# Two attention and FFN layers of a decode step: load sizes changed, and the last mean taken through the row sums of w_o

## Chip, core and metric

One core of a Trainium2 chip. The metric is the device time of one execution in microseconds (us). Engines are named as in the profile: PE (TensorE), PEld (its weight loads), DVE (VectorE), ACT (ScalarE), POOL (GpSimd), SP (SyncE, which issues all loads).

## The reference, cut to what matters

```python
def _layernorm(x, axis=-1, eps=1e-5):
    m = jnp.mean(x, axis=axis, keepdims=True); v = jnp.var(x, axis=axis, keepdims=True)
    return (x - m) / jnp.sqrt(v + eps)
def _A_ref(x, k_cache, v_cache, wq, wo):     # B=4, D=512, 32 heads, 8 KV heads, S=8192, Dh=128
    q = (x @ wq) as heads; k, v = each KV head repeated 4 times
    p = softmax(q k^T * Dh**-0.5);  return (p v, heads joined) @ wo
def _B_ref(x, w_gate, w_up, w_down):         # F=1792
    return (silu(x @ w_gate) * (x @ w_up)) @ w_down
x = x + _A_ref(_layernorm(x), ...);  x = x + _B_ref(_layernorm(x), ...)
x = x + _A_ref(_layernorm(x), ...);  x = x + _B_ref(_layernorm(x), ...)
```

Both layers use the same caches and weights. Everything is bf16, one token for each of 4 batches.

## The kernel before, in words

A unit is one KV head of one batch: 2 MB of K and 2 MB of V. There are 32 units a layer. On-chip memory has 8 slots of 2 MB (`kvf`, lines 202 to 203); layer 1 begins with the three units whose K and V are still there from layer 0 (`NRES`), so 122 caches of 2 MB are loaded in all. The list `items` (335 to 346) is the order of all loads, and `pump` (391) issues the next one on SP's queue as soon as its slot is free. Most caches come in one load of 2 MB. Those in `fours` (351) come in quarters of 512 KB: the last unit of each layer and the units 3 to 5 of layer 1's order, K and V both.

For each unit `keys` turns K in eight blocks (`turn`, DVE), makes the scores in eight blocks on PE (`scores`), and queues the softmax steps in the list `line`; `values` makes the products with V and queues what follows in the list `after`. Both lists are worked off between blocks (`advance`, `flush`). The last unit of a layer has V in the roles of weights, in eight blocks (`block_last`, 651): each block of 8 products waits for the piece of V it is in. Ahead of the last but one block the two lists are flushed (657 to 659): the row sums of p (`total`), and the rows of the unit before (`add_rows`, a product on PE and a step `scale_o` on DVE).

At the end of a layer `out_proj` (699) puts x into a PSUM bank by an identity product (`x_ahead`), picks the heads into `o4` and adds the 16 products with w_o. Then `center` (735) reduces the new x over its four column groups on DVE (`vs`), sums over the partitions by a product with ones into the bank `LNB`, and subtracts the mean from x (`xn`). `warm` puts in products whose result nobody reads. `ffn` (816) makes gate and up (4 x 14 products each), the activation, and down.

The FFN weights lie in slots 6 and 7 and a little room behind them. w_down comes in seven blocks of 256 rows (387); a partition gets 2 consecutive rows, so the columns of gate and up are taken in steps of 2 elements (833 and 834). In layer 0, as `ffn` has used a quarter slot's worth of weights, it issues the next quarter of the two K that follow (841 to 843, 884 to 895). In layer 1 the first two units' K slots are handed on by `quarter` (436): after every second score block (564) a quarter of the load that comes next into that slot is issued. For layer 1 the last quarters of w_gate and w_up are kept on chip (`park`, `keep`, `kept_at`) and the first three of w_up stay where they are, so only three quarters of w_gate and w_down are loaded again.

PE's, DVE's and ACT's instructions are recorded in program order and played at the end (`roll`, 898), with the repeating middle of a layer in a hardware loop; each engine runs its own list in order.

Of the kernel before, what the change touches and what calls it, by code (L numbers as in the profile page):

```python
# [146 lines left out]
def bass_interleave_layers__gqa_block_cached__swiglu_ffn__decode_kernel(  # L147
# [45 lines left out]
    with ExitStack() as es:  # L193
# [18 lines left out]
        wd_sb = kvf[:, f1:f1 + FO * D].rearrange("p (f n) -> p f n", f=FO)  # L212
        places = [f"s{s}.{q}" for s in range(NKEEP, NSLOT) for q in range(NB)]
        room = lambda a, b: places[(a - f0) // (TB * Dh):(b - 1 - f0) // (TB * Dh) + 1]
        at_w = {"wg": room(f0, f0 + FR * F), "wg3": room(f2, f2 + F), "wu": room(f3, f3 + F),
                **{("wd", j): room(f1 + 2 * j * D, f1 + (2 * j + 2) * D) + [f"wd{j}"] for j in range(FO // 2)}}
# [13 lines left out]
        rstd = sb("rstd", [P, B], FP32)  # L230
        o4 = sb("o4", [P, REP, B], BF16)
# [31 lines left out]
        def few(ap):  # L263
# [13 lines left out]
        sem_l = [sem(f"sem_l{q}") for q in range(NQ)]  # L277
        sem_h = [[sem(f"sem_h{k}{i}") for i in range(NQ)] for k in range(2)]
        sem_p = [sem(f"sem_p{i}") for i in range(7)]
        sem_x = sem("sem_x")  # L280
        sem_w = {n: [sem(f"sem_{n}{i}") for i in range(c)]
                 for n, c in (("wq", KT), ("wo", 1), ("wg", KT), ("wu", KT), ("wd", FO // 2))}
# [68 lines left out]
        fours = {(L, unit_order[L][-1]) for L in range(2)} | {(1, u) for u in unit_order[1][NRES:2 * NRES]}  # L351
# [19 lines left out]
        def load_weight(name, i=0):  # L371
# [11 lines left out]
            elif name == "wu":  # L383
                for k in range(KT):
                    T.dma("sp", [(wu_sb[k], runs(B_w_up[k * P:(k + 1) * P, :]))], sem_w["wu"][k], writes=[f"wu{k}"])
            else:
                for j in range(FO // 2):
                    T.dma("sp", [(wd_sb[:, 2 * j:2 * j + 2, :].rearrange("p e n -> p (e n)"),
                                  runs(B_w_down[2 * j * P:(2 * j + 2) * P, :]))], sem_w["wd"][j], writes=[f"wd{j}"])

        def pump():
            while issued[0] < len(items):
# [19 lines left out]
                if it in split:  # L412
                    n = NB // NQ
                    for q in range(NQ):
                        part(it, s, q * n, (q + 1) * n, sem_l[q])
                elif (L, u) in fours:
                    part(it, s, 0, NB, sem_s[s])
# [3 lines left out]

        def part(it, s, a, b, sem_):
            kind, L, u = it
            assert (L, u) in fours
            n = NB // NQ
            w, m = n * TB * Dh, S // NQ
            src = (A_k_cache if kind == "K" else A_v_cache)[u % B, u // B, :, :]
            T.dma("sp", [(kv[:, s, q * w:(q + 1) * w], runs(src[q * m:(q + 1) * m, :])) for q in range(a // n, b // n)],
                  sem_, writes=[f"s{s}.{k}" for k in range(a, b)])
# [6 lines left out]
        def quarter(it, i):  # L436
            to = heirs[it]
            if i == 0:
                place(to, slot_of[it])
            n = NB // NQ  # L440
            part(to, slot_of[it], i * n, (i + 1) * n, sem_h[unit_order[1].index(it[2])][i])

        def finished(it):
# [5 lines left out]
            elif it in heirs:  # L449
                quarter(it, NQ - 1)  # L450
# [102 lines left out]
        def keys(L, u):  # L553
            def block(q):
# [9 lines left out]
                if ("K", L, u) in heirs and (q + 1) % (NB // NQ) == 0 and q < NB - 1:  # L564
                    quarter(("K", L, u), q // (NB // NQ))
# [10 lines left out]
            if (L, i) == (1, B - 1):  # L576
                steps = steps[2:]
            ahead = unit_order[1][i + 2] if L == 1 and i in (1, 2) else u
# [8 lines left out]
        def values(L, u):  # L587
# [63 lines left out]
            def block_last(q):  # L651
# [5 lines left out]
                if q == NB - 2:  # L657
                    flush(line)
                    flush(after)
                warm({NB - 4: 3, NB - 2: 2}.get(q, 0), spare)  # L660
# [21 lines left out]
            if all((L, g * B + k) in done for k in range(B)):  # L682
                rest.append([0.5, None, lambda: out_proj(g, u != unit_order[L][-1])])
                if u != unit_order[L][-1]:
                    rest.append([1.3, None, add_to_x])


# [11 lines left out]
        def out_proj(g, more):  # L699
# [18 lines left out]
            for nt in range(KT):  # L718
                for c in range(REP):
# [3 lines left out]
                         stop=(c == REP - 1 if more else nt * REP + c == KT * REP - 1))  # L723

# [10 lines left out]
        def center(n, m, made=None):  # L735
            src, key = (xT[:], "x") if made is None else (bank(made)[:, 0:XB], f"pb{made}")
            T.op("dve", lambda e: e.tensor_reduce(vs[:], src.rearrange("p (k b) -> p b k", b=B), AX.X, ALU.add),
                 reads=[key], writes=["vs"])
# [3 lines left out]
            T.pe(bank(LNB)[:, 0:B], ones, vs[:], start=True, stop=True,  # L742
# [278 lines left out]
```

## Time and profile before

| | us |
|---|---|
| Median of 3 runs (lowest to highest) | 644.43 (643.29 to 644.66) |
| The profiled execution, its own time | 644.37 |
| Its span in the profile | 642.5 |
| PE, PEld, DVE, ACT, POOL busy | 515.2, 334.9, 450.7, 122.0, 19.3 |
| DMA: moved, mean rate over the span | 273.30 MB, 425 GB/s |
| Loads of 2048 KB: count, issue to landing (K, V) | 56 and 56, 28.9 and 32.7 |
| Loads of 512 KB of K and V: count, issue to landing | 20 and 20, 8.4 and 11.6 |
| Loads of w_down, 256 KB: count, issue to landing | 14, 18.3 |

The DMA row of the page gives the busy share of the 16 DMA engines in 40 slices of 16 us each. A timeline line has start, length, engine, line of the code, operation, written tile <- read tile with shapes, count, and in brackets the idle time ahead with what ended it. The helpers at lines 100, 118 and 136 record nearly all PE, DVE/ACT and DMA instructions, so one tells them apart by tiles and not by lines. The trace also has landing records: a load reports from each of the 16 DMA engines, and has landed with the last report.

### The profile page before, as it was taken

To read this page: it belongs to the slowest core of one execution; us is meant where nothing else is said; L and a number is where in the kernel's file an instruction comes from. 1 tells how busy PE (TensorE), PEld (TensorE's weight loads), DVE (VectorE), ACT (ScalarE), POOL (GpSimd) and SP (SyncE) were. 2 spreads that over 40 slices of the span, in tenths; PEclk is the share of its full clock that TensorE was granted. 3 is DMA by queue.
4 is the path that set the end of the run, shared out by engine and by line. 5 is a ranking of instruction groups with operands and counts; after the bars stand their busy time and mean duration, and the time that the engine had idled before them with its cause. 6 is when DMAs were issued, how large, how long until landed. Compare 5 with 4: busy or idle time off the path is not lost.

```text
span 642.5 us, 13067 instructions
## 1 busy us (share of the span) xinstructions
PE 515.2 (80%) x5063; PEld 334.9 (52%) x5086; DVE 450.7 (70%) x1108; ACT 122.0 (19%) x401; POOL 19.3 (3%) x73
## 2 busy tenths in 40 slices
PE   1656797887979878797888889897868968988987
PEld 1424454554646545455556656564545535645655
DVE  2646666867867767768764759987776876758883
ACT  0111211212212212212221422221221221212222
POOL 0000000000000000000000000000000000000000
PEclk9977789978887897979998999998987989769799
DMA  8999999999999999999999999999999999999996
GB/s 351 433 423 428 440 431 428 435 433 435 429 437 430 433 430 437 429 435 430 433 419 420 423 435 429 430 436 428 433 433 439 428 430 433 439 428 433 424 430 287
DMA packets 12695, 273.30 MB, mean 425 GB/s; under 512 B 3032, under 2 KB 3040, under 8 KB 3040
## 3 DMA queue, kind: packets, MB, share of 16 engines
q1 hardware_dynamic: 12672, 272.98, 99.1%
q8 instruction: 16, 0.26, 0.2%
q14 instruction: 7, 0.06, 0.0%
HBM read 272.96 MB, written 0.00 MB: 425 GB/s over the span
## 4 chain that ended last, share of the span: by engine, by line
DMA 71%; PE 15%; DVE 9%; SPq 4%; issue 1%; ACT 0%; POOL 0%; DVEq 0%; POOLq 0%
DMA kvf<-in_A_k_cache_dram 57%; PE ps L100 15%; DMA kvf<-in_A_v_cache_dram 11%; DVE kvf L118 6%; SPq L136 4%; DMA kvf<-in_B_w_down_dram 2%; DVE acc L118 2%; DVE one L118 1%; DVE pT L118 0%; DVE m L118 0%; ACT pb L118 0%; POOL zq L492 0%; DVE oT L118 0%; ACT one L118 0%; SPq L134 0%
## 5 line engine op out<-in xcount | busy, mean ns | idle before, releaser
L118 DVE STREAM_TRANSPOSE kvf<-kvf 128x512 f32<-128x512 f32 x488 | 322.6, 686 | 87.1 <-DMA kvf<-in_A_k_cache_dram 87.1
L100 PE MATMUL ps<-kvf,zq 128*128 128x256 bf16 x2048 | 316.4, 297 | 16.6 <-DVE kvf L118 11.9
L100 PEld LDWEIGHTS ps<-kvf,zq 128*128 128x128 bf16 x2048 | 197.5, 108 | 78.3 <-DVE kvf L118 28.7
L118 ACT ACTIVATE pb<-m 1x128 f32<-1x128 f32 x64 | 19.7, 308 | 434.4 <-DVE m L118 434.1
L100 PE MATMUL ps<-kvf,pT 128*16 128x512 bf16 x992 | 66.6, 390 | 10.5 <-DVE rl L118 7.5
L118 DVE SCALAR_TENSOR_TENSOR acc<-ps,own,acc 128x128 f32<-128x128 f32 x186 | 65.2, 351 | 5.4 <-ACT acc L118 0.6
L100 PE MATMUL ps<-identf,one 128*1 128x128 f32 x64 | 17.6, 275 | 49.0 <-DVE one L118 48.8
L100 PEld LDWEIGHTS ps<-identf,one 128*1 128x1 f32 x64 | 5.1, 80 | 77.3 <-DVE one L118 72.9
L100 PEld LDWEIGHTS ps<-kvf,pT 128*16 128x16 bf16 x992 | 19.4, 89 | 40.0 <-issue 22.3
L118 DVE TENSOR_REDUCE one<-ps 128x1 f32<-128x256 f32 x64 | 26.0, 406 | 18.5 <-PE ps L100 18.3
L118 ACT ACTIVATE pb<-ps,one,rstd 128x256 bf16<-128x256 f32 x64 | 36.0, 563 | 2.1
L100 PEld LDWEIGHTS ps<-head,acc 128*128 128x128 f32 x124 | 21.5, 217 | 28.2 <-DVE acc L118 26.3
L492 POOL TENSOR_TENSOR zq<-scr,quad 128x64 bf16<-128x64 bf16 x62 | 18.1, 292 | 599.6 <-PE ps L100 478.5
L100 PE MATMUL ps<-head,acc 128*128 128x4 f32 x124 | 24.2, 266 | 14.8 <-DVE acc L118 14.7
L118 DVE RECIPROCAL rl<-ps 128x4 f32<-128x4 f32 x64 | 10.4, 163 | 35.4 <-PE ps L100 35.4
L100 PEld LDWEIGHTS ps<-one,pb 1*128 1x128 f32 x128 | 21.3, 207 | 26.3 <-ACT pb L118 22.8
L100 PE MATMUL ps<-one,pb 1*128 1x1 f32 x128 | 26.8, 276 | 9.1 <-ACT pb L118 9.1
L118 DVE STREAM_TRANSPOSE pT<-pb 128x256 bf16<-128x256 bf16 x64 | 26.0, 407 | 4.6 <-ACT pb L118 4.5
L100 PE MATMUL ps<-wq_sb 128*128 128x512 bf16 (+1 forms) x83 | 27.3, 399 | 2.0 <-issue 1.3
L100 PE MATMUL ps<-xn,wq_sb 128*128 128x32 bf16 x284 | 21.1, 181 | 6.6 <-DMA wq_sb<-in_A_wq_dram 6.0
L100 PEld LDWEIGHTS ps<-rsm,one 128*128 128x128 f32 x128 | 22.0, 215 | 4.0 <-ACT rsm L118 2.5
L100 PEld LDWEIGHTS ps<-o,wo_sb 128*128 (+1 forms) x256 | 19.7, 101 | 8.3 <-issue 4.6
(72 smaller groups left out, 254.7 us busy)
## 6 DMA issues: line engine op xcount, KB each, us to landing
kvf<-in_A_k_cache_dram SPq DMA_DIRECT2D x56, 2048.0 KB, 28.9
kvf<-in_A_v_cache_dram SPq DMA_DIRECT2D x56, 2048.0 KB, 32.7
kvf<-in_A_k_cache_dram SPq DMA_DIRECT2D x20, 512.0 KB, 8.4
kvf<-in_A_v_cache_dram SPq DMA_DIRECT2D x20, 512.0 KB, 11.6
wq_sb<-in_A_wq_dram SPq DMA_DIRECT2D x4, 1024.0 KB, 8.2
wo_sb<-in_A_wo_dram SPq DMA_DIRECT2D x8, 512.0 KB, 37.6
kvf<-in_B_w_down_dram SPq DMA_DIRECT2D x14, 256.0 KB, 18.3
kvf<-in_B_w_gate_dram SPq DMA_DIRECT2D x7, 448.0 KB, 17.9
```

Of the source, the lines that this page charges most:

```text
L100: return e.matmul(out, lhsT=lhsT if at is None else lhsT(place(at)), rhs=rhs, **kw)
L118: self.tape[engname].append((repr((name, args, kw)), lambda e, _: getattr(e, name)(*args, **kw), left, sig, None))
L136: ins = e.add_instruction(mybir.InstDMACopy(name=self.nc.get_next_instruction_name(), mode="Copy", queue="qSPDynamicHW", ins=e.lower_ap_dm ...
L492: T.op(eng, lambda e: e.tensor_tensor(dst, q4, m4_, ALU.mult), reads=keys_ + ["quad"], writes=["zq"])
```

## The change

**Loads.** A table `pieces` takes the place of `fours`: units 3 to 5 of layer 1 come in two halves of 1 MB (K and V), the last unit of layer 0 in a half and two quarters, the last of layer 1 in three quarters and two eighths. `quarter` becomes `succeed`, which issues a piece when the score blocks that lay in its room are done; in `ffn`, `give` does it by the weights' room. w_down comes in five blocks (4, 4, 4, 1 and 1 groups of 128 rows) in place of seven; a partition then gets 4 consecutive rows in the first three, and gate and up take their columns in steps of 4 elements there and of 1 in the last two.

**The last mean.** For layer 1 alone. In layer 0's `ffn` ACT sums the rows of w_o that belong to the last KV head (`sum_rows`, 4 instructions), and DVE splits the f32 sums in three bf16 parts (`split_sums`, 7 instructions, in layer 1 at its fifth unit). At the last but one V block `mean_ahead` reduces x as it is before the last projection and multiplies by ones into `LNB`; behind w_o's 16 products `mean_rest` adds 12 products of the parts, each as a column repeated 128 times, with `o4`. `center` then leaves out its reduction and its product with ones, and has one warming product of 256 columns in place of two of 512.

```diff
@@ -210,10 +210,14 @@
...
+        WD = [(0, 4), (4, 8), (8, 12), (12, 13), (13, 14)]
+        assert WD[-1][1] == FO
+        wd_of = lambda fo: next(j for j, (a, b) in enumerate(WD) if a <= fo < b)
         places = [f"s{s}.{q}" for s in range(NKEEP, NSLOT) for q in range(NB)]
...
         at_w = {"wg": room(f0, f0 + FR * F), "wg3": room(f2, f2 + F), "wu": room(f3, f3 + F),
-                **{("wd", j): room(f1 + 2 * j * D, f1 + (2 * j + 2) * D) + [f"wd{j}"] for j in range(FO // 2)}}
+                **{("wd", j): room(f1 + a * D, f1 + b * D) + [f"wd{j}"] for j, (a, b) in enumerate(WD)}}
         wq_sb = sb("wq_sb", [P, KT, HqDh], BF16)
@@ -228,6 +232,9 @@
...
+        ws = sb("ws", [P, 2, REP], FP32)
+        ws3 = sb("ws3", [P, 3, REP], BF16)
         o4 = sb("o4", [P, REP, B], BF16)
@@ -348,7 +355,9 @@
...
         heirs = {("K", 1, unit_order[1][k]): items[ends[0] + 3 + k] for k in range(2)}
-        fours = {(L, unit_order[L][-1]) for L in range(2)} | {(1, u) for u in unit_order[1][NRES:2 * NRES]}
...
+        pieces = {(0, unit_order[0][-1]): (4, 2, 2), (1, unit_order[1][-1]): (2, 2, 2, 1, 1),
+                  **{(1, u): (4, 4) for u in unit_order[1][NRES:2 * NRES]}}
         issued = [0]
@@ -384,9 +393,9 @@
...
             else:
-                for j in range(FO // 2):
-                    T.dma("sp", [(wd_sb[:, 2 * j:2 * j + 2, :].rearrange("p e n -> p (e n)"),
-                                  runs(B_w_down[2 * j * P:(2 * j + 2) * P, :]))], sem_w["wd"][j], writes=[f"wd{j}"])
+                for j, (a, b) in enumerate(WD):
+                    T.dma("sp", [(wd_sb[:, a:b, :].rearrange("p e n -> p (e n)"), runs(B_w_down[a * P:b * P, :]))],
+                          sem_w["wd"][j], writes=[f"wd{j}"])
@@ -410,35 +419,39 @@
...
                 if it in split:
-                    n = NB // NQ
-                    for q in range(NQ):
-                        part(it, s, q * n, (q + 1) * n, sem_l[q])
-                elif (L, u) in fours:
-                    part(it, s, 0, NB, sem_s[s])
+                    for i in range(len(pieces[L, u])):
+                        part(it, s, i, i + 1, sem_l[i])
+                elif (L, u) in pieces:
+                    part(it, s, 0, len(pieces[L, u]), sem_s[s])
                 else:
...
+        def bounds(it, i):
+            n = pieces[it[1:]]
+            return sum(n[:i]), sum(n[:i + 1])
...
             kind, L, u = it
-            assert (L, u) in fours
-            n = NB // NQ
-            w, m = n * TB * Dh, S // NQ
             src = (A_k_cache if kind == "K" else A_v_cache)[u % B, u // B, :, :]
-            T.dma("sp", [(kv[:, s, q * w:(q + 1) * w], runs(src[q * m:(q + 1) * m, :])) for q in range(a // n, b // n)],
-                  sem_, writes=[f"s{s}.{k}" for k in range(a, b)])
+            w, m = TB * Dh, S // NB
+            at = [bounds(it, i) for i in range(a, b)]
+            T.dma("sp", [(kv[:, s, c * w:d * w], runs(src[c * m:d * m, :])) for c, d in at], sem_,
+                  writes=[f"s{s}.{k}" for c, d in at for k in range(c, d)])
...
-        def quarter(it, i):
+        def succeed(it, k):
...
             to = heirs[it]
-            if i == 0:
+            if to not in slot_of:
                 place(to, slot_of[it])
-            n = NB // NQ
-            part(to, slot_of[it], i * n, (i + 1) * n, sem_h[unit_order[1].index(it[2])][i])
+            for i in range(len(pieces[to[1:]])):
+                if bounds(to, i)[1] == k + 1:
+                    part(to, slot_of[it], i, i + 1, sem_h[unit_order[1].index(it[2])][i])
@@ -561,8 +574,8 @@
...
                     deviation(lsc_sb, "lsc")
-                if ("K", L, u) in heirs and (q + 1) % (NB // NQ) == 0 and q < NB - 1:
-                    quarter(("K", L, u), q // (NB // NQ))
+                if ("K", L, u) in heirs and q < NB - 1:
+                    succeed(("K", L, u), q)
                 if q == NB // NQ and L == 1 and first:
@@ -575,6 +588,8 @@
...
                 steps = steps[2:]
+            if (L, i) == (1, B):
+                split_sums()
             ahead = unit_order[1][i + 2] if L == 1 and i in (1, 2) else u
@@ -657,6 +672,8 @@
...
                     flush(after)
+                    if L == 1:
+                        mean_ahead()
                 warm({NB - 4: 3, NB - 2: 2}.get(q, 0), spare)
@@ -680,10 +697,38 @@
...
             if all((L, g * B + k) in done for k in range(B)):
-                rest.append([0.5, None, lambda: out_proj(g, u != unit_order[L][-1])])
+                rest.append([0.5, None, lambda: out_proj(g, u != unit_order[L][-1], L == 1)])
                 if u != unit_order[L][-1]:
...
+        def sum_rows(g):
+            for c in range(REP):
+                T.op("act", lambda e: e.activation(bank(TOT)[:, 0:D], wo_sb[:, g, c, :], ACTF.Copy, accum_out=ws[:, 0, c:c + 1]),
+                     reads=["wo3"], writes=[f"pb{TOT}", "ws"])
...
+        def split_sums():
...
+            left, part_ = ws[:, 0, :], ws[:, 1, :]
+            for k in range(3):
+                T.op("dve", lambda e: e.tensor_copy(ws3[:, k, :], left), reads=["ws"], writes=["ws3"])
+                if k < 2:
+                    T.op("dve", lambda e: e.tensor_copy(part_, ws3[:, k, :]), reads=["ws3"], writes=["wsp"])
+                    T.op("dve", lambda e: e.tensor_tensor(left, left, part_, ALU.subtract), reads=["ws", "wsp"], writes=["ws"])
...
+        def mean_ahead():
...
+            T.op("dve", lambda e: e.tensor_reduce(vs[:], xT[:].rearrange("p (k b) -> p b k", b=B), AX.X, ALU.add),
+                 reads=["x"], writes=["vs"])
+            T.pe(bank(LNB)[:, 0:B], ones, vs[:], start=True, stop=False, reads=["vs", "onesf"], writes=[f"pb{LNB}"])
...
+        def mean_rest():
...
+            for k in range(3):
+                for c in range(REP):
+                    T.pe(bank(LNB)[:, 0:B], ws3[:, k, c:c + 1].to_broadcast([P, P]), o4[:, c, :], start=False,
+                         stop=(k == 2 and c == REP - 1), reads=["ws3", "o4"], writes=[f"pb{LNB}"],
+                         sig=(k == 2 and c == REP - 1))
@@ -721,6 +766,8 @@
...
                          stop=(c == REP - 1 if more else nt * REP + c == KT * REP - 1))
+            if sums and not more:
+                mean_rest()
@@ -732,15 +779,17 @@
...
-        def center(n, m, made=None):
+        def center(n, m, made=None, summed=False):
             src, key = (xT[:], "x") if made is None else (bank(made)[:, 0:XB], f"pb{made}")
-            T.op("dve", lambda e: e.tensor_reduce(vs[:], src.rearrange("p (k b) -> p b k", b=B), AX.X, ALU.add),
-                 reads=[key], writes=["vs"])
+            if not summed:
+                T.op("dve", lambda e: e.tensor_reduce(vs[:], src.rearrange("p (k b) -> p b k", b=B), AX.X, ALU.add),
+                     reads=[key], writes=["vs"])
             if made is not None:
...
             warm(m, SBK[0])
-            T.pe(bank(LNB)[:, 0:B], ones, vs[:], start=True, stop=True,
-                 reads=["vs", "onesf"], writes=[f"pb{LNB}"])
+            if not summed:
+                T.pe(bank(LNB)[:, 0:B], ones, vs[:], start=True, stop=True,
+                     reads=["vs", "onesf"], writes=[f"pb{LNB}"])
             warm(n, SBK[0])
@@ -787,11 +836,11 @@
...
-        def kept_at(name, f=None):
+        def kept_at(name, f=None, n=1):
...
             a = {"wg": 0, "wu": G - 1}[name] * w
-            return a if f is None else wq_sb[:, f // w, a + f % w:a + f % w + 2 * P - 1:2]
+            return a if f is None else wq_sb[:, f // w, a + f % w:a + f % w + n * (P - 1) + 1:n]
@@ -820,8 +869,16 @@
...
             ks = items[ends[0] + 1:ends[0] + 3]
-            n = NB // NQ
-            size = n * TB * Dh
+            rooms = [(k, NKEEP + n, i, n * SL + bounds(k, i)[1] * TB * Dh) for n, k in enumerate(ks)
+                     for i in range(len(pieces[k[1:]]))]
...
+            def give(a, b):
...
+                for n, (k, s, i, end) in enumerate(rooms):
+                    if a < end <= b:
+                        if i == 0:
+                            place(k, s)
+                        part(k, s, i, i + 1, sem_p[n])
             for (w_sb, wname, bk) in ((wg_sb, "wg", gb), (wu_sb, "wu", ub)):
@@ -830,8 +887,9 @@
...
                     for fo in range(FO):
-                        f = fo // 2 * 2 * P + fo % 2
-                        w = kept_at(wname, f) if kt == FR and last else w_sb[kt][:, f:f + 2 * P - 1:2]
+                        a, b = WD[wd_of(fo)]
+                        f, n = a * P + fo - a, b - a
+                        w = kept_at(wname, f, n) if kt == FR and last else w_sb[kt][:, f:f + n * (P - 1) + 1:n]
                         T.pe(out[:, fo, :, :], w, few(xn[:, kt * B:(kt + 1) * B]),
@@ -839,8 +897,7 @@
...
                 if bk == gb and not last:
-                    place(ks[0], NKEEP)
-                    part(ks[0], NKEEP, 0, (f1 - f0) // size * n, sem_p[0])
+                    give(0, f1 - f0)
             T.op("dve", lambda e: e.tensor_tensor(fb(gr), fb(gT), rb, ALU.mult),
@@ -867,7 +924,7 @@
...
                              start=(fo == i == 0), stop=(fo == (BOTH if i == 2 else FO) - 1),
-                             reads=["hT"] + at_w["wd", fo // 2], writes=[f"pb{k}"], sig=(fo == (BOTH if i == 2 else FO) - 1))
+                             reads=["hT"] + at_w["wd", wd_of(fo)], writes=[f"pb{k}"], sig=(fo == (BOTH if i == 2 else FO) - 1))
                     if fo == BOTH - 1:
@@ -875,24 +932,16 @@
...
             park("wg")
+            sum_rows(unit_order[1][-1] // B)
             for fo in range(FO):
...
                          start=False, stop=(fo == FO - 1 and nt == KT - 1),
-                         reads=["hT"] + at_w["wd", fo // 2], writes=[f"pb{OUTB}"], sig=(nt == KT - 1 and fo % 2 == 1))
-                i = (f1 - f0 + (fo + 1) * D) // size
-                if i > (f1 - f0 + fo * D) // size:
...
-                    if i <= NQ:
-                        part(ks[0], NKEEP, (i - 1) * n, i * n, sem_p[i - 2])
-                        if i == NQ:
-                            place(ks[1], NKEEP + 1)
-                    else:
-                        part(ks[1], NKEEP + 1, (i - NQ - 1) * n, (i - NQ) * n, sem_p[i - 2])
-                        if fo == FO - 1:
-                            part(ks[1], NKEEP + 1, (i - NQ) * n, (i - NQ + 1) * n, sem_p[5])
-                            part(ks[1], NKEEP + 1, NB - n, NB, sem_p[6])
+                         reads=["hT"] + at_w["wd", wd_of(fo)], writes=[f"pb{OUTB}"], sig=(nt == KT - 1 and fo % 2 == 1))
+                at = f1 - f0 + fo * D
+                give(at, at + D)
+            give(at + D, 2 * SL)
@@ -979,7 +1028,10 @@
...
             flush(after)
-            center(2, 2, OUTB)
+            if L == 1:
+                center(0, 1, OUTB, True)
+            else:
+                center(2, 2, OUTB)
             rows = ffn(L == 1)
```

## The prediction

> **What bounds the kernel now.** I read the page's slices and DMA queues first, then the windows of 20 us, then the chain of the last 60 us, then the timeline of the last 12. The DMA row and its queue say that the 16 DMA engines are never idle:
>
> ```profile
> DMA  8999999999999999999999999999999999999996
> GB/s 351 433 423 428 440 431 428 435 433 435 429 437 430 433 430 437 429 435 430 433 419 420 423 435 429 430 436 428 433 433 439 428 430 433 439 428 433 424 430 287
> ...
> q1 hardware_dynamic: 12672, 272.98, 99.1%
> q8 instruction: 16, 0.26, 0.2%
> ```
>
> The reader sees 99.1% of the span in packets of one queue, and a dip to 419 to 423 GB/s in slices 21 to 23 (321 to 369 us), the change of layers, where the 512 KB and 256 KB pieces are. So before the last loads only a cheaper stream of transfers can save time: an engine that works there is covered. The chain of the end says where that stops:
>
> ```profile
> 614.42 16.40 DMA kvf<-in_A_v_cache_dram
> 630.82 0.05 issue
> 630.87 2.49 PE ps L100 x55
> 633.36 0.02 issue
> 633.38 0.19 DVE o L118
> 633.57 0.04 issue
> 633.61 0.79 PE ps L100 x17
> 634.40 0.04 issue
> 634.45 0.62 PE ps L100 x3
> 635.07 0.16 issue
> 635.22 5.13 PE ps L100 x141
> ```
>
> From 630.82, when the third quarter of the last V lands, to 642.5 it is TensorE and short VectorE steps, not DMA. The fourth quarter lands at 632.04 by the landing records. The last w_down pair lands at 639.69 and is used at about 640.1, so the weights are not late.
>
> **Own time.** The profiled execution took 644.37 us, of which the span is 642.5; the median shown is 644.43 (643.29 to 644.66), so the two agree. I make the sum against 644.37. About 0.2%, 1.3 us, is what a measurement of this kernel can tell from no change.
>
> **Term 1, the loads.** 191 transfers become 175. Up to the third quarter of the last V there are 15 fewer: 12 in the six units of layer 1 (quarters to halves), 2 in layer 0's last K and V, 2 in layer 0's w_down, and one more in layer 1's last K. What one costs I take from the landing records, by the last engine to report. Whole 2 MB loads land every 4.847 us (418.63 to 602.82 in 38 steps), quarters every 1.227 (351.36 to 368.54 in 14), so 4.908 a unit: three more transfers cost 0.061, 0.020 each. Six units give -0.25, layer 0's last pair -0.04, the last K +0.02. w_down's 256 KB blocks land every 0.627; three of 512 KB at 1.227 and two of 128 KB at 0.327 (half the step from 512 to 256 taken off 0.627, an estimate) make 4.34 in place of 4.39: -0.05. Sum **-0.32**. The other end is the packets' own durations: 32 KB take 1.217 us, 16 KB 0.621, so a unit in halves would save 0.10 and the term would be -0.85 with the 9 ns signal packets. The near end is 0: the last V's matmuls wait about 0.45 us for the third quarter, but if VectorE's chain before them (busy 11.6 of the 11.7 us from 612.8 to 624.5) moves less than the loads, part is lost. I take the landing spacing, since it is the thing itself.
>
> Later starts of halves: at the change of layers a half is requested after four score blocks where a quarter was after two, some 1.2 us later. The records say that this is covered. When the first such V quarter was requested (353.35), the queue held data until 358.69; the K behind it (357.57) found data until 363.6; the smallest lead I find is 5 us. VectorE's transposes of the two first loads ran at 352.3 to 360 and behind; the halves that they need would be there by 351.3, 353.7, 356.2 and 358.6, each before its transposes. If that cover failed, the queue would run dry for at most 1.2 us.
>
> **Term 2, the row sums.** Four ScalarE reductions of 128x512 have no row of their own; a 128x256 takes 0.56 with 0.19 for reading the sum, so four of them are 3 to 5 us. ScalarE does nothing between the exponential at 341.03 and 352.36; price 0. The seven 128x4 VectorE steps of the split stand before the reduction at 376.93, where VectorE was idle 1.18; at about 0.2 each they push it by some 0.3, under a DMA lead of 8 us. Price 0. Without these covers: 4 us and 1.4 us.
>
> **Term 3, the new wait.** The sum of x as it is before the last projection is now made at the last but one V block, ahead of that block's products. In program order TensorE has: row sums of p, rows of the second last unit, the new product of the sums of x (which waits for VectorE), a warming product, then the last 16 V products. Everything in TensorE's queue stands behind that wait. The timeline prices it:
>
> ```profile
> 631.28 0.36 PE L100 MATMUL ps<-rsm,one 128*128 128x4 f32 x2
> ...
> 631.51 0.36 PE L100 MATMUL ps<-head,acc 128*128 128x4 f32 x2
> ...
> 631.73 0.38 PE L100 MATMUL ps<-wq_sb 128*128 128x512 bf16 x1
> 631.91 0.17 DVE L118 TENSOR_TENSOR oT<-ps,rl 128x4 bf16<-128x4 f32 x1
> ...
> 632.09 0.56 PE L100 MATMUL ps<-pT,kvf 128*128 128x32 bf16 x16
> ```
>
> The new VectorE reduction stands behind the step at 631.91, which itself needs the product at 631.51. Back-to-back small steps start 0.09 apart (634.22, 634.31): it starts at 632.00. From such a reduction to the product on it is 0.23 (634.22 to 634.45): 632.23. From that to the next warming product 0.24 (634.45 to 634.69): 632.47. From a warming product to what follows 0.22 (346.38 to 346.60): the V products start at 632.69, not 632.09. **+0.60.** The split of the fourth quarter in eighths, which alone would let half of the 16 products (0.2 us) run before the last landing, gives nothing then: at 632.69 both eighths are there.
>
> **Term 4, the mean.** Before, from w_o's first product (633.61):
>
> ```profile
> 633.61 0.57 PE L100 MATMUL ps<-o,wo_sb 128*128 128x32 bf16 x16 [0.29 <-DVE o L118]
> ...
> 634.22 0.17 DVE L118 TENSOR_REDUCE vs<-ps 128x4 f32<-128x16 f32 x1 [0.66 <-PE ps L100]
> ...
> 634.45 0.38 PE L100 MATMUL ps<-vs,one 128*128 128x4 f32 x2
> ...
> 634.95 0.18 DVE L118 SCALAR_TENSOR_TENSOR xn<-ps,xT 128x16 bf16<-128x16 f32 x1 [0.47 <-PE ps L100]
> ```
>
> VectorE gets the projection 0.61 after that start and xn 1.34 after. Now 12 products of 128x4 follow the 16. Sixteen picks of 128x4 bf16 take 0.41 (632.92), 25.6 ns each; 12 are 0.31, and xn starts 0.61 + 0.31 = 0.92 after. **-0.42.** The copy of x runs beside them. Their weights are one column repeated 128 times, which no bf16 row shows. The far bound is a pass of the f32 product with repeated ones, 0.12 (0.24 for two): 12 would be 1.44, a loss of 0.7. I take 25.6 ns, from the same output and type.
>
> **Term 5, strides of gate and up.** w_down's blocks of four make 96 of the 112 gate and up products of the last stage load weights in steps of 8 bytes; before it was 4. At 4 bytes 28 products go in 0.71 (635.19 to 635.90), 25 ns each; unstrided, 16 in 0.39, 24 ns. Picks of 32 columns in steps of 16 bytes take 25.6. So 0, with a far bound of four such loads for 128 columns, 102 ns: 96 x 77 ns = +7.4. The nearest row is that at 4 bytes: I take 0. Layer 0's products would be under the DMA lead.
>
> The Trainium skill, in "SBUF — State Buffer" (the passage on cachelines, under the port swizzle), says that accesses within a 16-byte line run at full rate if a line is hit at least twice, and that each new line otherwise costs. By that, 8 bytes still hit a line twice and the sum stays; at 4 bytes the trace agrees (25 ns beside 24), and no row here shows 8.
>
> **Sum:** -0.32 + 0 + 0.60 - 0.42 + 0 = -0.14: 644.37 - 0.14 = **644.2 us**, within 0.2%.
>
> **Rivals.**
> - *The transfers are worth their packets, and the new wait is not paid.* -0.85, no +0.60, -0.2 for the eighths, -0.42: -1.5, **642.9**. For it: the dip of slices 21 to 23 (420 against 433 GB/s over 48 us is 1.4 us). Against: the landing spacing, and the program order that puts the wait ahead of the V products. Also here: the last engine reports 3.57 us after the first at 632.04, and gained 1.5 us of that at each of two instruction loads (33.2, 368.8). Should these fall elsewhere in the new program, 0.3 to 1.5 goes; should a third fall on it, 1.5 comes.
> - *Strided weights are slower* (the other side). Place: gate and up, 635.2 to 638.3, straight on the path. If a load takes twice 25 ns, 96 x 25 = +2.4: **646.6**. It decides from about 15 ns each (1.45 us). For it: no row at 8 bytes with 128 columns. Against: 4 bytes cost nothing.
> - *The change does nothing:* fewer transfers do not bring the last V forward, since VectorE's chain holds it; +0.60 - 0.42: **644.6**, within 0.2% too.
>
> **Chances.** Forecast 0.46, nothing 0.10: within 0.2% together 0.56. Rival one and the fetches' luck 0.20: faster. Strides 0.16, dearer column products or a third fetch 0.08: slower 0.24. The likeliest case's own range is 643.5 to 644.9. The range to hold 8 in 10 reaches to rival one and to doubled strided loads: 642.7 to 646.6; about 0.08 lies below and 0.10 above.
>
> **What would show it.** Third quarter of the last V landed at about 630.5; a unit in halves landing in about 4.86 us. A reduction of xT on VectorE right behind the oT step, TensorE waiting for it some 0.3 us, and the last 16 V products in one run, some 1.87 us after the third quarter (before 1.27). xn 0.92 after w_o's first product. Gate and up at 25 ns a product. From that landing to the end 11.85 us (before 11.67). It is wrong if the last V products do not wait for VectorE, if gate and up stretch, or if the DMA row shows a slice below 9 at the change of layers.

## The result, and the profile after

The changed kernel takes **653.13 us** (median of 5 runs, 651.65 to 654.64), the kernel before 644.43 (643.29 to 644.73): a ratio of 1.0139, 95% interval 1.0119 to 1.0159. The forecast was 644.2 with a range to 646.6: the time is 8.9 above the one and 6.5 above the other. The profiled execution of the changed kernel took 653.13, of which the span is 651.3.

The prediction ended with signs that would show it wrong. The DMA row of the page of the changed kernel (busy tenths in 40 slices, now of 16.3 us) shows one of them:

```profile
DMA  8999999999999999999996999999999999999995
GB/s 363 442 416 431 438 432 437 429 437 423 441 429 433 437 427 441 427 433 431 433 415 278 391 438 425 436 426 441 429 431 435 429 437 431 435 431 433 423 427 222
...
q1 hardware_dynamic: 11904, 272.98, 97.8%
```

The slice from 342 to 358 us is at 6 and 278 GB/s; the slice of before at that place is at 9 and 420. The same bytes now fill 97.8% of the span, not 99.1%: the queue was empty for some us. The windows (length, then busy time of PE, PEld, DVE, ACT, POOL, then granted TensorE clock, DMA share, GB/s) give place and length, first one row of the kernel before and then the changed kernel:

```profile
350.00:352.00 2.00, 1.77 (x51) 1.15 (x50) 0.95 (x7) 0.00 (x0) 0.00 (x0) 1.00 1.01 426
```

```profile
350.00:352.00 2.00, 0.00 (x0) 0.00 (x0) 0.00 (x0) 0.00 (x0) 0.00 (x0) 0.50 0.42 180
352.00:354.00 2.00, 0.93 (x18) 0.66 (x19) 0.00 (x0) 0.00 (x0) 0.00 (x0) 0.50 0.00 0
354.00:356.00 2.00, 1.78 (x25) 1.10 (x23) 0.26 (x2) 0.00 (x0) 0.00 (x0) 0.50 0.00 0
356.00:358.00 2.00, 2.00 (x41) 1.06 (x41) 0.79 (x5) 0.00 (x0) 0.00 (x0) 0.50 0.85 262
```

The DMA time that is missing from these four rows is 2 x 0.58 + 4 + 2 x 0.15 = 5.5 us. The other engines stand as well: none of them runs anything from 350 to 352. The timelines of PE and of SP's queue there say why:

```profile
346.21 0.38 PE L100 MATMUL ps<-wq_sb 128*128 128x512 bf16 x1
353.07 0.40 PE L100 MATMUL ps<-scr,kvf 128*128 128x32 bf16 x8 [6.49 <-DMA kvf<-in_A_k_cache_dram]
```

```profile
340.26 16.27 SPq L136 DMA_DIRECT2D kvf<-in_A_k_cache_dram  x4
```

Products of w_down (tiles `scr` for h, `kvf` for the weights), the fourth run of eight in layer 0's FFN (eight products are two groups, here groups 6 and 7), stand 6.49 us, and what ends that is the landing of a half of **K**, a load that they do not read. By the landing records that half lands at 353.03; w_down's last block had landed at 347.82. SP's queue has four K halves to issue from 340.26 on, and gets the last one off only at 356.5. They land at 350.68, 353.03, 360.52 and 364.54.

The end of the chain of the changed kernel, to hold against the one shown of before:

```profile
620.18 16.42 DMA kvf<-in_A_v_cache_dram
...
637.85 0.09 DVE vs L118
...
637.99 2.45 PE ps L100 x37
...
640.74 1.17 PE ps L100 x29
...
642.07 6.55 PE ps L100 x137
```

The third quarter of the last V lands at 636.60, was 630.82: +5.78. From it to the end of the span there are 14.70 us, were 11.68: +3.02. Together they are 8.80, the difference of the spans as the page rounds them (651.3 and 642.5). So there are two losses, one far from the end and one at it. In the second, `vs`, the new reduction of x, stands in the chain as predicted, and the last run of PE (gate, up and down) is 6.55 long, was 5.13.

### The profile page after: what moved, and what is told of

The parts are those of the page before. It is cut to its first block, busy times and chain, and to the rows that moved or that the text cites. A ratio compares the mean times of both kernels' runs of the same rounds, so it can differ in the third digit from the quotient of the medians.

```text
span 651.3 us, 13087 instructions
## 1 busy us (share of the span) xinstructions
PE 513.4 (79%) x5074; PEld 335.0 (51%) x5097; DVE 452.0 (69%) x1115; ACT 124.8 (19%) x409; POOL 19.3 (3%) x73
## 3 DMA queue, kind: packets, MB, share of 16 engines
q1 hardware_dynamic: 11904, 272.98, 97.8%
## 4 chain that ended last, share of the span: by engine, by line
DMA 71%; PE 17%; DVE 8%; SPq 2%; issue 1%; ACT 0%; DVEq 0%; POOL 0%; POOLq 0%
DMA kvf<-in_A_k_cache_dram 57%; PE ps L100 17%; DMA kvf<-in_A_v_cache_dram 11%; DVE kvf L118 5%; DMA kvf<-in_B_w_down_dram 3%; SPq L136 2%; DVE acc L118 1%; DVE one L118 1%; DVE pT L118 0%; DVE m L118 0%; ACT pb L118 0%; DVE ws L118 0%; DVE oT L118 0%; POOL zq L505 0%; SPq L134 0%
## 5 line engine op out<-in xcount | busy, mean ns | idle before, releaser
L100 PE MATMUL ps<-kvf,zq 128*128 128x256 bf16 x2048 | 312.6, 294 | 17.2 <-DVE kvf L118 9.2
L100 PEld LDWEIGHTS ps<-kvf,zq 128*128 128x128 bf16 x2048 | 194.7, 107 | 78.2 <-DVE kvf L118 30.3
L100 PE MATMUL ps<-kvf,pT 128*16 128x512 bf16 x992 | 66.1, 387 | 11.7 <-DVE rl L118 7.6
L100 PE MATMUL ps<-o,wo_sb 128*128 128x32 bf16 x256 | 23.8, 182 | 0.7 <-DVE o L118 0.6
```

What stands on the lines that cost most here:

```text
L100: return e.matmul(out, lhsT=lhsT if at is None else lhsT(place(at)), rhs=rhs, **kw)
```

## The experiments

Each ratio is to the kernel before, timed beside the experiment on the same chip; its medians there were 644.12 (experiments 1 to 4), 643.70 (5, 7, 8 and 11) and 643.60 (6, 9, 10 and 12). The changed kernel's 653.13 was taken beside 644.43. The ratio is not that of the two medians, and where two intervals overlap the difference between two experiments is not clear of the noise. A trace shows one execution.

**Theory.** PE's wait is a false one. Each w_down product is recorded as reading the room of its whole block (`at_w["wd", j]`). That room is counted in eighths of a slot, 1024 columns each. Counted from slot 6, block 1 (groups 4 to 7) lies in columns 7424 to 9472 and so touches `s6.7` (7168 to 8192), which of these four only groups 4 and 5 use. After group 5, which ends at 8448, `give` issues the second half of K into slot 6 and becomes the writer of `s6.7`; group 6, whose own rows start at 8448, then waits for that half. Before, groups 6 and 7 were a block of their own, from 8448 on. **Rival:** the halves are just requested too late (four score blocks and not two), as Term 1 had weighed.

**1. Each product reads its own 128 rows' room.** All else as changed.

```diff
+        own_w = lambda fo: room(f1 + fo * D, f1 + (fo + 1) * D) + [f"wd{wd_of(fo)}"]
-                         reads=["hT"] + at_w["wd", wd_of(fo)], ...
+                         reads=["hT"] + own_w(fo), ...
```

> Changed kernel, but each w_down product in both FFNs names only the room of its own 128 rows, not that of its whole block of four. Theory A (a wait that no data needs: the products of w_down's 7th group stand behind the landing of the second K half, the K load that waits for the 14th group is issued late, the DMA queue runs dry between 353 and 358 us): the wait of 6.5 us on K is gone, no slice below 9 at the change of layers, the third quarter of the last V lands at 630 to 632 in place of 636.6, the time is 646 to 648 with the slow TensorE clock at the end (0.5 from about 640), 644 to 645 if that clock is a consequence of the hole and comes back. Theory B (the halves themselves come too late, requested after four blocks in place of two): the hole stays, 652 to 654. Theory C (strided weight loads): 652 to 653, gate and up at more than 30 ns a product at full clock.

Measured: 645.90 (644.62 to 646.43, 11 runs), ratio 1.0024 [1.0015, 1.0033], 7.2 under the changed kernel and 0.1 below the 646 to 648 expected with the slow clock, which its trace has (0.50 from 636 to 640). Its page:

```profile
DMA  8999999999999999999999999999999999999996
```

No slice is below 9 but the first and the last. The third quarter of the last V lands at 630.80, was 636.60 in the changed kernel. The theory holds; the halves as such do not run the queue dry.

**2. The wait alone, in the kernel before.** The products of group 6 in layer 0 also read `s6.7`.

```diff
-                         reads=["hT"] + at_w["wd", fo // 2], ...
+                         reads=["hT"] + at_w["wd", fo // 2] + (["s6.7"] if fo == 6 else []), ...
```

> Kernel before with one edit: in layer 0 the products of w_down's 7th group of rows also wait for the room into which the fourth K quarter has just been requested. Theory A: a wait of 6 to 7 us on that quarter appears, the queue runs dry, the third quarter of the last V lands 5 to 7.5 us later, 649.5 to 652. Theory B or C: at most 1 us slower, 644.4 to 645.5.

Measured: 650.05 (649.23 to 651.98, 5 runs), ratio 1.0089 [1.0075, 1.0103]. Its page:

```profile
DMA  8999999999999999999997999999999999999997
```

One dependency too many, with the old loads and the old mean, costs 5.9 us and makes the same hole. So it suffices.

That leaves 1.8 us of experiment 1 over the kernel before. The next two part it.

**3. Experiment 1 without the new mean** (loads and strides only).

> As e1, and the mean of layer 1 made as in the kernel before (no row sums, no 12 products, reduction and product with ones behind the projection). Theory A: 643.5 to 644.5, some 0.3 us under the kernel before, its last stage as before (11.7 us from the third quarter of the last V to the end). If the blocks of w_down or their strides cost something of their own: 646 or more, with the last stage 13 us or more.

Measured: 645.00 (643.71 to 645.93, 11 runs), ratio 1.0013 [1.0004, 1.0022]. That is above the 643.5 to 644.5 of theory A, and not the 646 of the other branch. The profiled execution, 643.71, is the lowest of the eleven.

**4. The new mean alone** (loads in quarters, w_down in seven blocks, as before).

> All loads in the sizes of the kernel before (quarters of 512 KB, w_down in seven blocks of 256 rows), with the mean through the row sums as in the changed kernel. Theory A, with the new wait costing what its terms say: no hole, 644.5 to 645 (+0.2 at the end: V products 0.6 later, mean 0.4 sooner). If the slow clock of the last stage comes from the mean's path (waiting, and fewer warming products): 646.5 to 648, granted clock about 0.5 in the last 8 us. Theory B and C say nothing against either.

Measured: 645.79 (643.72 to 646.69, 6 runs), ratio 1.0025 [1.0011, 1.0039]. This lies between the two expectations, and the six executions are in two groups: 643.72 and 643.90, and four from 645.67 to 646.69. The trace is of the lowest, 643.72, with a granted clock of 1.00 to the end of PE's work, so it does not show what the four others have. In it the V products start 1.85 after the third quarter (before 1.27) and xn comes 0.96 after w_o's first product (before 1.34): from the one term +0.58, from the other -0.38. From that quarter to the end of the span there are 12.0 us (before 11.7). By the medians experiments 3 and 4 are 0.9 and 1.7 over the kernel before, more together than the 1.8 that they were to part; their intervals reach some 0.6 and 0.9 to either side.

**5. Experiment 3 with w_down in seven blocks of 256 rows** (so steps of 4 bytes, and no false wait either).

```diff
-        WD = [(0, 4), (4, 8), (8, 12), (12, 13), (13, 14)]
+        WD = [(j, j + 2) for j in range(0, FO, 2)]
```

> The loads of K and V as changed (halves and eighths), but w_down in seven blocks of 256 rows as before, so gate and up load weights in steps of 4 bytes, and the mean as before. If steps of 8 bytes cost some 7 ns a product (theory), gate and up are back to about 3.1 us in place of 3.9, and the time is that of the loads alone as they are, less 0.8: about 644.1, 0.0 to 0.4 under the kernel before. If the steps cost nothing and the halves themselves are late somewhere (rival), it stays at 644.8 to 645.2.

Measured: 643.95 (643.02 to 645.02, 11 runs), ratio 0.9997 [0.9988, 1.0006]. Experiment 3 and this one differ in w_down's blocks alone: 1.05 in the medians, though taken on two chips, 0.42 of it by the kernel before, and the intervals just overlap. So the price is read from the timelines of the last gate and up, first experiment 3's, then this one's:

```profile
635.90 1.51 PE L100 MATMUL ps<-xn,kvf 128*128 128x32 bf16 x42
637.26 0.60 PE L100 MATMUL ps<-xn,wq_sb 128*128 128x32 bf16 x14
```

```profile
636.44 1.20 PE L100 MATMUL ps<-xn,kvf 128*128 128x32 bf16 x42
637.49 0.50 PE L100 MATMUL ps<-xn,wq_sb 128*128 128x32 bf16 x14
```

From the start of a row of 42 to the start of the next is 1.36 with blocks of four groups (32.4 ns each) and 1.05 with pairs (25.0). Both are at full clock. By the starts of single products it is 33 ns at steps of 8 bytes and 25 for the two groups with columns side by side.

**6. A ladder of steps.** The kernel before, other column steps in the last gate and up.

```diff
-                        f = fo // 2 * 2 * P + fo % 2
-                        w = kept_at(wname, f) if kt == FR and last else w_sb[kt][:, f:f + 2 * P - 1:2]
+                        n = {("wg", 0): 1, ("wg", 1): 2, ("wg", 2): 4, ("wu", 0): 8, ("wu", 1): 12, ("wu", 2): 6}.get((wname, kt), 2) if last else 2
+                        f = min(fo // n * n * P, F - n * P) + fo % n
+                        w = kept_at(wname, fo // 2 * 2 * P + fo % 2) if kt == FR and last else w_sb[kt][:, f:f + n * (P - 1) + 1:n]
```

> The kernel before, and in the last FFN alone the products of gate and up load their weights in other steps of columns: gate steps of 1, 2 and 4 elements (2, 4 and 8 bytes) and then 2 for the quarter kept on chip, up steps of 8, 12 and 6 elements (16, 24 and 12 bytes) and then 2; the columns are then not those of the reference, so gate and up are other numbers. If the step sets the price (theory: 25 ns at 4 bytes, 32 at 8): 24 to 25, 25 and 32 ns a product, and more, 40 or above, from 12 bytes on. If what cost 32 ns was something else in that kernel, such as the clock or a DMA into the same slots (rival), all stand at 25.

Measured: 646.06 (one run; in its last FFN gate and up do not take the reference's columns). Its timeline:

```profile
635.79 0.61 PE L100 MATMUL ps<-xn,kvf 128*128 128x32 bf16 x14
636.24 0.50 PE L100 MATMUL ps<-xn,wq_sb 128*128 128x32 bf16 x14
636.59 2.48 PE L100 MATMUL ps<-xn,kvf 128*128 128x32 bf16 x42
638.91 0.54 PE L100 MATMUL ps<-xn,wq_sb 128*128 128x32 bf16 x14
```

The 14 products in steps of 8 bytes take 0.45 to the next row, 32 ns each; the 14 behind them, at 4 bytes, 0.35, 25 each. The 42 are three sizes; by the starts of single products they go at 60 ns (16 bytes), 58 (24) and 47 (12). The clock fell to half amid them, at 637.62, so 12 bytes were seen at half clock alone. But 24 bytes go at 58 on both sides of the fall, and the last 14, at 4 bytes and half clock, take only 27, so the clock is not what sets these prices. The theory holds, the rival falls.

**7. Experiment 1 with the reduction of x early**, at the last unit's first V block.

> The changed kernel with each w_down product reading only its own rows' room, and in it the reduction of x moved from the last but one V block to the first one; the product with ones stays where it is. If TensorE's wait for that reduction is worth 0.60 (theory), the last V products end about 1.4 after the third quarter of the last V in place of 1.85, and the time falls from 645.9 to about 645.3. Rival: the wait also lets the clock fall to half at the end, and with it gone the clock stays up: then gate and up take 3.9 in place of 4.1 and the down products less, and the time falls to about 644.5. If neither holds it stays at 645.9.

Measured: 645.53 (644.53 to 646.72, 10 runs), ratio 1.0025 [1.0016, 1.0034], no change from experiment 1 (1.0024). The expected price did not come, and the timeline says why:

```profile
632.05 0.39 PE L100 MATMUL ps<-vs,one 128*128 128x4 f32 x2 [0.26 <-DVE oT L118]
```

The wait only has a new name: 0.26 for `oT`, was 0.34 for `vs`. The product writes bank `LNB`, and the step on `oT` still reads that bank (`scale_o(LNB, SW)`). The V products start 1.76 after the third quarter (632.51 - 630.75), not 1.4.

**8. Experiment 7 with both warming products of 512 columns** (`center(2, 2, OUTB, True)`). The expectation counts them double: there is one ahead of where the product with ones was and one behind.

> The kernel before this one with the two warming products of 512 columns in front of xn and the two behind put back (the change had one of 256). If the fewer warming products are what lets the clock fall in the last stage (theory), most executions keep the full clock there: about 644.6, against 645.3. If the clock does not hang on them (rival), the time is that of the kernel without them, or up to 0.2 longer.

Measured: 644.55 (644.11 to 647.62, 12 runs), ratio 1.0021 [1.0010, 1.0032]. The median falls by 1.0, as the theory has it, but the ratio falls by 0.0004 only and the two intervals overlap (seven executions are at 644.11 to 644.58, five at 645.35 to 647.62): inconclusive by itself. What its trace does show is the price of the clock. The same two us in experiment 7's profiled execution and in this one's:

```profile
638.00:640.00 2.00, 2.00 (x54) 1.80 (x53) 1.29 (x5) 0.19 (x1) 0.00 (x0) 0.50 0.20 72
```

```profile
638.00:640.00 2.00, 2.00 (x54) 1.92 (x53) 0.53 (x3) 0.00 (x0) 0.00 (x0) 1.00 0.04 10
```

Experiment 7's is at half clock from 635.01 to 641.83, and its gate and up take 4.13 us and what stands behind them 5.27. This one's is at full clock, and the same two stretches take 3.91 and 4.13.

**9. Fewer warming products in the kernel before.**

```diff
-            center(2, 2, OUTB)
+            center(*((0, 1) if L == 1 else (2, 2)), OUTB)
```

> The kernel before, with the last center's two warming products of 512 columns replaced by one of 256, as the change does, and nothing else. If fewer warming products let the clock fall in the last stage (theory), many executions show half the clock from there on and the time is 1 to 2 longer: 645 to 645.7. If the clock hangs on the stand before the last V products or on the weights' steps (rival), it is within 0.3 of the kernel before, at best 0.2 under it.

Measured: 644.66 (643.72 to 646.27, 11 runs), ratio 1.0018 [1.0008, 1.0027]. So leaving them out costs about 1.1 us by itself, a little below the 645 to 645.7 expected. The windows of its profiled execution, and then of experiment 5, same two us:

```profile
634.00:636.00 2.00, 1.70 (x50) 1.73 (x51) 0.61 (x4) 0.32 (x2) 0.00 (x0) 0.59 0.85 344
```

```profile
634.00:636.00 2.00, 1.80 (x45) 1.53 (x45) 0.68 (x5) 0.08 (x1) 0.00 (x0) 1.00 0.98 392
```

The granted clock is 0.59 against 1.00. That fewer warming products cost time is measured. That they do it through the clock is not shown: the profiled execution, 643.72, is the lowest of the eleven, and with half clock from 634.37 to 637.79 it takes 12.0 us from the third quarter to the end (before 11.7). And warming products are not the only thing on which the clock hangs: in experiment 6, with both warming products in place, it was 0.50 from 632 to 634.

**10. The changed kernel with w_down alone in seven blocks.**

> The changed kernel with w_down alone put back into seven blocks of 256 rows; halves and eighths of K and V and the mean through the row sums stay as changed. If the blocks of four groups are what makes the change slow (theory: the wait for a later K -7.2, the steps of 8 bytes -0.8 to -1.0), 644.8 to 645.2, 8 under the changed kernel, and DMA 9 in all slices at the change of layers. If the wait had another source (rival), a slice stays below 9 and the time above 648.

Measured: 644.37 (643.35 to 645.50, 11 runs), ratio 1.0008 [0.9999, 1.0017]. This is 0.4 below the lower end of what was expected. No slice is below 9 at the change of layers. One line of the change held nearly all of its loss.

**11. Halves, pairs, early reduction, both warming products.**

> All that looked good in one kernel: halves and eighths of K and V, w_down in seven blocks of 256 rows (steps of 4 bytes, and no wait for a later K), the reduction of x early, the mean through the row sums, and the warming products of before. If the prices add up (loads -0.3, mean -0.3 to -0.4, no new wait, no stride): 643.4 to 643.6, faster than the kernel before by 0.1%. If the mean through the row sums costs by itself, through the clock or the 12 products (rival): 644.5 or more.

Measured: 644.16 (643.44 to 646.37, 12 runs), ratio 1.0005 [0.9995, 1.0015]. This lies between the two expectations: neither price can be told.

**12. Experiment 11 with the product of the sums behind the picks of the heads**, where PE waits for DVE anyway.

> The kernel of halves, pairs, early reduction and both warming products, and the product of the sums of x with ones moved behind the picks of the heads, where TensorE stands 0.28 us for VectorE anyway. If the 0.26 us that it stood before the last V products came from the bank which the step on oT still read (theory), the last V products are 1.4 after the third quarter of the last V, and the time falls by 0.4 to 0.5: 643.4 to 643.7, against 643.2 to 643.5 of the better runs of the kernel before. If the time of this end hangs on the clock alone (rival), it stays at 644.2, or rises, as 0.24 us of f32 products come out of the stretch that keeps the clock up.

Measured: 643.73 (643.02 to 644.45, 11 runs), ratio 1.0001 [0.9992, 1.0010]. Its timeline:

```profile
631.37 0.38 PE L100 MATMUL ps<-wq_sb 128*128 128x512 bf16 x1
631.58 0.55 PE L100 MATMUL ps<-pT,kvf 128*128 128x32 bf16 x16
...
632.75 0.39 PE L100 MATMUL ps<-vs,one 128*128 128x4 f32 x2
```

Nothing waits ahead of the V products any more (they start 1.12 after the third quarter, which landed at 630.46; 1.4 was expected, 1.27 is the kernel before), and the product on `vs` has no wait either. The median is 0.4 under experiment 11's, as expected, but the intervals overlap. The time is that of the kernel before: the change in its best form gains nothing that can be measured.

## Why the prediction was wrong, step by step

**Term 1, the loads: the step that failed is its cover**, "The records say that this is covered" and "If that cover failed, the queue would run dry for at most 1.2 us". I had priced only the later request behind the score blocks. That cover held: in experiment 1 the queue is full. But the pieces of the first two K's are requested from within layer 0's FFN, between the products of w_down, and what these wait for I had not followed. The prediction had these four halves landed by 351.3, 353.7, 356.2 and 358.6; in the changed kernel the third landed at 360.52 and the fourth at 364.54, and in experiment 1, without the wait, at 356.38 and 359.41. A block of four groups takes `s6.7` into the room of groups 6 and 7; groups 6 to 13 then stand until a K half lands, and the next half is requested only after group 13. The price is 7.2 us in the medians (experiment 1), 5.78 in the two traces at the third quarter, against a term of -0.32, and the queue ran dry for 5.5 us and not 1.2. The wait needed no run to be found: PE's order has it, at an instruction that the change touched only through a list of names. I had looked for new waits where the change adds an operation, and not where it makes a name wider. The term's own arithmetic stands as far as it can be told: halves land 2.43 apart in experiment 1, 4.85 for a cache of 2 MB (predicted 4.86; the prediction's "unit" there, and its "six units", are single caches, K or V), and the loads without the false wait and the strides give 0.9997 [0.9988, 1.0006], in which -0.32 (0.9995) lies.

**Term 2, the row sums:** 0, and no run shows anything else: with them all done and the rest mended (experiment 12), the ratio is 1.0001. No run takes them out alone.

**Term 3, the new wait:** right in kind and size. +0.60 was predicted, 1.85 - 1.27 = +0.58 was seen at full clock (experiments 1 and 4). In the changed kernel itself it is 2.22, since the f32 product and the warming product behind it ran at half clock. What I named as its cause was half of it: with the reduction gone from there, the bank held the product back almost as long (experiment 7).

**Term 4, the mean:** -0.42 predicted; -0.29 in the changed kernel (641.79 - 640.74 = 1.05 against 1.34), -0.38 in experiment 4. Right in kind, and the 12 column products at the price of a pick hold (0.31 from 641.22 to 641.53). But the term counted the two warming products as mere delay. Without them the kernel before loses 1.1 (experiment 9): by these numbers the term should have been a loss.

**Term 5, strides:** 0 was taken, and the size is +0.8: 96 products x 8 ns = 0.77; 3.90 for gate and up in experiment 3 against 3.10 in experiment 5. The rival "strided weights are slower" had the mechanism, at 0.8 and not the 2.4 of a doubled load. The Trainium skill ("SBUF — State Buffer", the passage on cachelines) says that two hits on a 16-byte line are enough for the full rate; by that, steps of 8 bytes are free. The measurement differs and decides: 33 ns against 25. What agrees is that the line is what counts: 128 columns in steps of 16 or 24 bytes touch 128 lines and take 60 and 58 ns, 96 lines (12 bytes) 47, 64 lines (8 bytes) 33. By these numbers that is about 0.5 ns a line (an estimate), with a floor of 25 at which 32 lines (4 bytes) lie.

**Not in the sum: the clock.** All steps at the end were taken at the clock of the trace of before, 1.00 until 640. In the changed kernel's windows it is half from 638 to 648; the first of them:

```profile
638.00:640.00 2.00, 2.00 (x24) 1.50 (x24) 0.17 (x1) 0.00 (x0) 0.00 (x0) 0.50 1.05 443
```

The +3.02 after the third quarter are: V products' start +0.95 (Term 3's 0.58, the rest at half clock), from there to w_o +0.40, to xn -0.29, gate and up +1.01 (strides 0.8), from their end on +0.94, with 0.01 in rounding and issue. At full clock the same stretches of the changed program are 1.85 and 1.51 (experiment 1), 0.96 and 0.28 (experiment 4), 3.91 for gate and up and 4.13 behind them (experiment 8): 12.6 in place of 14.7. So about 2 us of it is the clock, and the rest is Term 3's wait and the strides, less Term 4's gain. What brings the clock down may be the wait, the fewer warming products or both. Experiments 8 and 9 speak for the warming products in their times, experiment 7 does not tell on the wait, and what share each has stays open. The Trainium skill ("TensorE: Matmul & The Clock Gate", Part 1) tells of a free-running window of some 3.4 us, after an idle one of which the clock is halved. The traces agree on the windows: in the clock records of the fourteen traces the stretches between two changes of the clock are all whole multiples of 3.41 us (in the changed kernel half clock from 637.97 to 648.21, 10.24), and they lie elsewhere in each execution. That fits one and the same stage at 1.00 in one trace and at 0.50 in another. The traces do not agree on the idle window: here a stage that is only partly idle is enough (PE busy 1.89 and 1.29 in the two stretches of 2 us ahead of 638).

**The range** reached to 646.6, the doubled strided loads; its only empty queue was the 1.2 us of Term 1, which stood neither in the sum nor in a rival. The sign "a slice below 9 at the change of layers" was the right one to watch.

## What to carry to other kernels

When tiles grow, ask what else their dependency names now cover: a wait is decided by the granularity at which reads and writes are recorded, and a block that spans a boundary inherits the waits of both sides. Follow it for the instructions between which loads are issued, above all, since there a wait turns into an empty queue, which nothing later gave back in this kernel. And a filler product on the critical path is to be priced by taking it away from the old kernel, not by its duration.

## What the runs showed of the hardware

- Products of gate and up, with weights of 128 bf16 columns, go by the 16-byte lines that the columns touch. From start to start they take 25 ns at steps of 2 and 4 bytes, 33 at 8, 47 at 12, 60 at 16 and 58 at 24. At half clock 4 bytes take 27 and 8 bytes still 33: these products hardly feel the clock. The f32 product with ones between two of them took 223 ns at full clock (248 from start to start, less 25) and 427 at half (454 less 27).
- With PE standing from 346.6 to 353.07 the granted clock of the changed kernel was 0.92 in 347 to 348 and 0.50 from 348 on; it was back at 0.96 only in 358 to 359, 5 us after PE's work had begun again. By the clock records the half clock lasted from 347.84 to 358.08, 10.24 us or three times 3.41.
- Sixteen DMA engines that run dry for 5.5 us move the third quarter of the last V by 5.8: this kernel's queue was in use for 99.1% of the span before, and what was lost was not caught up.
